# States kept as 64 by 48 blocks per head, with states and outputs computed in 64x64 array tiles

## The chip, the cores and the metric

The kernel runs on one core of a Trainium2 chip. The metric is the device time of one execution in microseconds (us). A run that is more than 1.5% above the fastest run of the same kernel is called slow here, the others fast, and ratios use fast runs alone.

Engine names in the profile lines: PE is the matrix engine (TensorE), PEld its weight loads, DVE is VectorE, ACT is ScalarE, POOL is GpSimd, SP is SyncE. A "q" behind the name means the sequencer of that engine, as when it issues a DMA. L929 is line 929 of the kernel that the profile belongs to.

## The reference

Two parts follow each other. Gated linear attention keeps a 48 by 48 state for each batch and head, and a dense block with a squared ReLU follows. All inputs and outputs are fp32. The sizes are B = 4 batches, H = 8 heads, S = 768 steps, D = 48.

```python
state = np.zeros((B, H, D, D))
for t in range(S):
    state = alpha[:, :, t, :, None] * state + einsum('bhd,bhe->bhde', k[:, :, t], v[:, :, t])
    y[:, :, t] = einsum('bhd,bhde->bhe', q[:, :, t], state)
x = y.transpose(0, 2, 1, 3).reshape(3072, 384)
h = np.maximum(x @ w_in, 0.0)          # w_in 384 x 2048
out = (h * h) @ w_out                  # w_out 2048 x 384
```

## The kernel before

The 3072 tokens are worked off in 12 units of 256 tokens: 3 stages in time, 4 batches in each. Within a unit, the recurrence is written as matrix products. For each unit TensorE computes, in this order: the decays (sums of log alpha), transposes of q and k, the scores, then one "output block", then the two large dense products of the MLP (L929 with `w_in`, L965 with `w_out`). A list scheduler in Python fixes the order of the instructions on each engine when the kernel is built. A list called `ORDER` tells it in which order the attention parts come, and it fits the dense work of earlier units in between.

The change and the argument are about the output block. It has up to three parts: "inter" (q times the state so far), "PM x V" (masked scores times v), and the state products k times v of the next unit. In the kernel before, two heads form a pair. Keys of a pair fill 128 rows of the array, so the product k times v of a pair is 128 by 96, of which only the two 48 by 48 blocks on the diagonal are wanted. A multiply with the mask `own` clears the rest. TensorE uses array tiles of 128x64 for inter and of 64x128 for the other two:

```python
def state_mm(g):                      # next states: 64x128 tiles, 96 columns
    ...
    for p in range(NPR):              # 4 pairs of heads
        for j in range(2):
            for c in range(1 if last else 2):
                h0 = 64 * c
                ins = pe.matmul(banks[c][:, p * 96:p * 96 + 96],
                                QKS[qs][h0:h0 + 64, 0, j, 2 * p:2 * p + 2, :].rearrange("p h d -> p (h d)"),
                                VBF[vb][h0:h0 + 64, 2 * p:2 * p + 2, j, :], ...)

def output_mm(g):
    ...
    for c in range(2):                # inter: 128x64 tiles, 96 columns
        state = SMD[x2] if c else SBD[sr]
        ...
        for p in range(NPR):
            for j in range(2):
                pe.matmul(psX[64 * j:64 * j + 64, c, p * 96:p * 96 + 96],
                          KQT[kt][:, 1, j, p, 64 * c:64 * c + 64], state[:, p * 96:p * 96 + 96], ...)
    for h in range(H):                # PM x V: 64x128 tiles, 48 columns
        for jk in range(2):
            for c in range(2):
                n, rr_ = h // 2, h % 2
                ins = pe.matmul(psX[:, c, h * D:(h + 1) * D],
                                PM[pm][64 * c:64 * c + 64, n // 2, rr_, n % 2, jk, :],
                                VBF[vb][64 * c:64 * c + 64, h, jk, :], ...)
...
# state update (DVE and POOL), 384 columns
add("dve", lambda e: e.tensor_tensor(TMP[0][:], ps0, SBD[sr][:], ALU.add), ...)
add("pool", lambda e: e.tensor_tensor(sm3, hd(TMP[0][:]), own, ALU.mult), ...)
...
ORDER = ["f0", "k0", "p0", "f1", "y0", "p1", "k1", "y1", "f2", "p2", "k2"]
for g in range(3, G):                 # f: front, p: scores, k: states, y: output,
    ORDER += [f"f{g}", f"w{g - 1}", f"p{g}"]     # w: output with the next unit's states
```

## Time and profile before

| | before |
|---|---|
| median of the timed runs | 179.53 us (179.25 to 180.75, 3 runs); 179.84 us with a fourth, run beside the changed kernel |
| span of the profiled execution | 179.8 us (its own time was 181.48 us, above all of the timed ones) |
| TensorE busy | 173.1 us, 96% |
| VectorE / ScalarE busy | 121.6 us / 118.8 us |
| matmuls, and as many weight loads | 2301 |
| first dense product | at 19.1 us |

These lines are from the page of before: busy time, share and number of instructions of each engine; the queue that fetches instructions, with packets, MB and share of the DMA engines' time; the chain of waits by engine; and two groups of instructions (line, engine, operation, tensors, shape, count, then busy us and mean ns of one, then the idle time before them).

```profile
PE 173.1 (96%) x2301; PEld 137.8 (77%) x2301; DVE 121.6 (68%) x192; ACT 118.8 (66%) x215; POOL 28.2 (16%) x36
...
q8 instruction: 18, 0.29, 0.7%
...
PE 85%; DMA 10%; SPq 2%; issue 1%; ACT 0%
...
L796 DVE TENSOR_TENSOR tmp<-psZ,sbd 128x384 f32<-128x384 f32 x8 | 4.4, 554 | 5.4 <-PE psZ L743 5.4
...
L770 PE MATMUL psX<-vbf,pm 64*128 64x48 bf16 x384 | 6.9, 180 | 0.0
```

TensorE is the bound: it is busy 96% of the time and has 85% of the chain. The state add on DVE takes 554 ns, but DVE is busy for only 68%. The line of q8 looks like a line to skip. It says that TensorE's instructions reached it in 18 packets of 16 KB (0.29 MB over 18). That q8 is TensorE's own queue is read from the counts: 4637 TensorE instructions in the trace go with 18 packets here, and 5265, 6033 and 6241 with 20, 23 and 24 in runs below, about one packet for every 256.

The next lines are the timeline of TensorE in before around one output block: start, length, engine, line, operation, tensors, array tile, shape, count.

```profile
93.01 0.60 PE L929 MATMUL psWH<-xt,win 128*128 128x256 bf16 x4
93.54 0.36 PE L763 MATMUL psX<-sbd,kqt 128*64 128x96 bf16 x8
93.74 0.34 PE L763 MATMUL psX<-smd,kqt 128*64 128x96 bf16 x8
94.01 0.58 PE L770 MATMUL psX<-vbf,pm 64*128 64x48 bf16 x32
94.42 0.50 PE L743 MATMUL psZ<-vbf,qks 64*128 64x96 bf16 x16
94.86 0.44 PE L929 MATMUL psWH<-xt,win 128*128 128x256 bf16 x2
```

Lengths overlap (one matmul of PM x V is recorded with some 180 ns, and the next pair starts 25 ns after it), so starts are what to compare. PM x V takes from 94.01 to 94.42, that is 32 matmuls in 0.41 us, 26 ns for each pair of tiles. The block has 64 matmuls. With the changes of array mode (by the starts, 94 ns at its head, 96 ns before PM x V and 93 ns at its end) it costs 1.47 us beyond the dense streams around it (in a dense stream a matmul of 256 columns follows every 109 ns in this trace, one of 384 columns every 162 ns).

The last lines are from the chain of waits of before, in order of time (start, length, what):

```profile
108.81 1.09 PE psWH L929 x11
109.91 3.92 DMA xt<-xbf
...
113.87 0.88 PE psWH L929 x6
```

In this execution the first dense product of unit 7 waits for a transpose made by DMA. TensorE stands still for 1.1 us at 112.6 us.

### The profile page before, as it was taken

To read this page: it belongs to the slowest core of one execution; us is meant where nothing else is said; L and a number is where in the kernel's file an instruction comes from. 1 tells how busy PE (TensorE), PEld (TensorE's weight loads), DVE (VectorE), ACT (ScalarE), POOL (GpSimd) and SP (SyncE) were. 2 spreads that over 40 slices of the span, in tenths; PEclk is the share of its full clock that TensorE was granted. 3 is DMA by queue.
4 is the path that set the end of the run, shared out by engine and by line. 5 is a ranking of instruction groups with operands and counts; after the bars stand their busy time and mean duration, and the time that the engine had idled before them with its cause. 6 is when DMAs were issued, how large, how long until landed. Compare 5 with 4: busy or idle time off the path is not lost.

```text
span 179.8 us, 5243 instructions
## 1 busy us (share of the span) xinstructions
PE 173.1 (96%) x2301; PEld 137.8 (77%) x2301; DVE 121.6 (68%) x192; ACT 118.8 (66%) x215; POOL 28.2 (16%) x36
## 2 busy tenths in 40 slices
PE   7989899999999999999999999799999999999994
PEld 5868698866787788878878788678878788788773
DVE  6569488698877997997998829773728745424130
ACT  4673399478767859949888639756549554656441
POOL 3250750022020021323405300500000000000000
PEclk9999999999999999999999999999999999999999
DMA  5999999999999999999999999756122941130112
GB/s 127 278 250 193 227 264 211 237 270 252 215 281 225 272 269 189 300 234 319 247 180 284 232 246 266 179 104 146 46 55 60 142 44 47 44 91 0 44 47 88
DMA packets 74871, 32.39 MB, mean 180 GB/s; under 512 B 70336, under 2 KB 73536, under 8 KB 74848
## 3 DMA queue, kind: packets, MB, share of 16 engines
q1 hardware_dynamic: 71344, 27.34, 67.3%
q0 software_dynamic: 3504, 4.72, 14.0%
q8 instruction: 18, 0.29, 0.7%
q14 instruction: 5, 0.04, 0.1%
HBM read 25.17 MB, written 4.72 MB: 166 GB/s over the span
## 4 chain that ended last, share of the span: by engine, by line
PE 85%; DMA 10%; SPq 2%; issue 1%; ACT 0%
PE psWH L929 36%; PE psO L965 33%; DMA win<-in_moe_w_in_dram 5%; PE psX L770 3%; DMA raw<-in_alpha_dram 3%; PE psX L763 3%; DMA xt<-xbf 2%; PE psZ L743 2%; PE psX L826 2%; SPq L511 2%; PE psX L899 1%; PE psZ L826 1%; PE psX L872 1%; PE psWH L630 1%; PE psO L1009 1%
## 5 line engine op out<-in xcount | busy, mean ns | idle before, releaser
L929 PE MATMUL psWH<-xt,win 128*128 128x256 bf16 x576 | 74.1, 275 | 1.8 <-DMA xt<-xbf 1.0
L929 PEld LDWEIGHTS psWH<-xt,win 128*128 128x128 bf16 x576 | 65.1, 145 | 7.0 <-DMA xt<-xbf 1.3
L965 PE MATMUL psO<-wout,gt 128*128 128x384 bf16 x368 | 68.9, 326 | 0.1
L937 ACT ACTIVATE rr<-psWH 128x512 bf16<-128x512 f32 x86 | 51.1, 596 | 24.9 <-PE psWH L929 23.1
L965 PEld LDWEIGHTS psO<-wout,gt 128*128 128x128 bf16 x368 | 34.8, 98 | 18.3 <-ACT osb L972 0.3
L947 DVE TENSOR_TENSOR gt<-rr 128x1024 bf16<-128x1024 bf16 (+1 forms) x44 | 27.3, 627 | 29.0 <-ACT rr L937 28.7
L972 ACT ACTIVATE osb<-psO 128x384 f32<-128x384 f32 x23 | 11.3, 493 | 14.4 <-PE psO L965 14.0
L839 DVE TENSOR_TENSOR pm<-psZ,caus 128x1024 bf16<-128x1024 f32 x12 | 14.6, 1217 | 2.6 <-PE psZ L826 2.6
L839 DVE TENSOR_TENSOR pm<-psX,caus 128x1024 bf16<-128x1024 f32 x12 | 14.6, 1218 | 1.7 <-PE psZ L826 1.5
L857 ACT ACTIVATE xbf<-psX 128x768 bf16<-128x768 f32 x11 | 8.9, 809 | 8.7 <-PE psZ L743 6.5
L951 ACT ACTIVATE gt<-rr 128x1024 bf16<-128x1024 bf16 (+1 forms) x16 | 13.9, 866 | 0.5 <-DVE rr L939 0.2
L623 POOL TENSOR_TENSOR prd<-raw 128x384 f32<-128x384 f32 x7 | 7.4, 1063 | 37.4 <-DMA raw<-in_alpha_dram 37.4
L1009 PE MATMUL psO<-zero 128*128 128x256 bf16 x74 | 11.7, 306 | 1.3 <-DVE zero L426 1.3
L693 DVE TENSOR_TENSOR qks<-raw,ek 128x768 bf16<-128x768 f32 x11 | 11.3, 1030 | 0.0
L693 DVE TENSOR_TENSOR qks<-raw,eq 128x768 bf16<-128x768 f32 x11 | 10.8, 985 | 0.0
L1009 PEld LDWEIGHTS psO<-zero 128*128 128x128 bf16 x74 | 7.6, 109 | 2.8 <-DVE zero L426 1.2
L689 POOL CAST vbf<-raw 128x768 bf16<-128x768 f32 x5 | 5.0, 995 | 20.2 <-DMA raw<-in_v_dram 20.2
L796 DVE TENSOR_TENSOR tmp<-psZ,sbd 128x384 f32<-128x384 f32 x8 | 4.4, 554 | 5.4 <-PE psZ L743 5.4
L939 DVE TENSOR_SCALAR rr<-psWH 128x512 bf16<-128x512 f32 x10 | 6.9, 689 | 1.3 <-PE psWH L929 0.9
L770 PE MATMUL psX<-vbf,pm 64*128 64x48 bf16 x384 | 6.9, 180 | 0.0
L770 PEld LDWEIGHTS psX<-vbf,pm 64*128 64x128 bf16 x384 | 5.6, 93 | 0.8
L642 ACT ACTIVATE ek<-psWH 128x384 f32<-128x384 f32 x10 | 4.9, 490 | 2.0 <-PE psWH L634 1.8
(118 smaller groups left out, 165.4 us busy)
## 6 DMA issues: line engine op xcount, KB each, us to landing
out_dram<-osb SPq DMA_DIRECT2D x23, 192.0 KB, 2.7
raw<-in_k_dram SPq DMA_DIRECT2D x11, 384.0 KB, 4.8
raw<-in_q_dram SPq DMA_DIRECT2D x11, 384.0 KB, 5.4
raw<-in_v_dram SPq DMA_DIRECT2D x10, 384.0 KB, 5.5
raw<-in_alpha_dram SPq DMA_DIRECT2D x10, 384.0 KB, 4.2
win<-in_moe_w_in_dram POOLq DMA_DIRECT2D x2, 768.0 KB, 9.7
wout<-in_moe_w_out_dram POOLq DMA_DIRECT2D x2, 768.0 KB, 9.2
raw<-in_alpha_dram SPq DMA_DIRECT2D x2, 192.0 KB, 3.2
```

The costliest lines, as they stand in the source:

```text
L623: alts={"pool": (lambda e: e.tensor_tensor(hd(PRD[la][:]), al(0), al(1), ALU.mult), pool_ns(HD))})
L693: add("dve", lambda e, a=a, E=E: e.tensor_tensor(QKS[qs][:, a, :, :, 0:D], RAW[r][:, 1 + a].rearrange("p h j d -> p j h d"), E[la][:].rear ...
L770: ins = pe.matmul(psX[:, c, h * D:(h + 1) * D], PM[pm][64 * c:64 * c + 64, n // 2, rr_, n % 2, jk, :], VBF[vb][64 * c:64 * c + 64, h, jk, ...
L839: add("dve", lambda e, hf=hf, psT=psT: e.tensor_tensor(PM[pm][:, hf].rearrange("p r n j t -> p (r n) (j t)"), psT[:, :, :].rearrange("p r ...
L857: add("act", lambda e: e.activation(XBF[x2][:], psX[:, :, 0:HD], AF.Copy), act_ns(2 * HD), p0 + 6100, reads=[("ps", "X", 0), ("ps", "X", 1 ...
L929: ins = pe.matmul(psH[hb][:, i * T:(i + 1) * T], WIN[:, kk, hidden(fj)], mov, start=(kk == 0), stop=(kk == KT - 1))
L937: add("act", lambda e, hb=hb, rr=rr: e.activation(rr, psH[hb], AF.Relu), act_ns(512), pu + 600, reads=[("ps", "H", hb)], writes=[("rr", rb ...
L947: add("dve", lambda e, dst=dst, sq=sq: e.tensor_tensor(dst, sq, sq, ALU.mult), 148 + k * 267, pu + 1200, reads=[("rr", rb, h) for h in ran ...
L951: "act": (lambda e, dst=dst, sq=sq: e.activation(dst, sq, AF.Square), act_ns(k * 512))})
L965: ins = pe.matmul(psS, GT[gt][:, fj, j, :], WOUT[:, fj, :], start=(fj == 0), stop=(fj == FT - 1))
L972: add("act", lambda e, ob=ob, psS=psS: e.activation(OSB[ob][:], psS, AF.Copy), act_ns(DM), ps_ + 700, reads=[keyS], writes=[("osb", ob)], ...
L1009: pr.fill(lambda pe: pe.matmul(psO[:, 0:256], ZERO[:, 0:128], ZERO[:, 0:256], skip_group_check=True), 109, min(o.start for o in pr.order[" ...
```

## The change

The intent is to spend no array time on the unwanted halves of the states. A state becomes a 64 by 48 block per head; the two heads of a pair stand above each other, so a state tile has 192 columns instead of 384, and the mask `own` is not needed. All three parts of the block run in 64x64 tiles, four at a time, which also saves the change of mode within the block (96 ns in the trace of before). The inter products are cut into two halves: in the second half each row tile uses the bank that the other one used in the first. A semaphore stands between the halves, and the next states are put in front of its wait, so that the wait costs little (in the four full blocks of after the next inter product starts 3 to 9 ns after the last state product).

In numbers, a full block goes from 64 matmuls to 128: inter 16 to 32, PM x V 32 to 64, states 16 to 32.

```diff
+    HS = HD // 2
-    PE_X = 7                                  # units from here on: x transposed by DMA
+    DMA_X = (8, 9, 10)
-    DENSE = {}
+    DENSE = {11: 11 * 13000 + 15500}
-    SBD = sb("sbd", [128, HD], BF16, 2 * B)
-    SMD = sb("smd", [128, HD], BF16, 2)
+    SBD = sb("sbd", [128, HS], BF16, 2 * B)
+    SMD = sb("smd", [128, HS], BF16, 2)
 ...                                           # selector matmul of the decays goes, v always cast on chip
 # states
-                    for c in range(1 if last else 2):
-                        ins = pe.matmul(banks[c][:, p * 96:p * 96 + 96], ...
+                    for c in range(halves):
+                        for x in range(2):
+                            ins = pe.matmul(banks[c][64 * x:64 * x + 64, p * D:p * D + D],
+                                            QKS[qs][h0:h0 + 64, 0, j, 2 * p + x, :],
+                                            VBF[vb][h0:h0 + 64, 2 * p + x, j, :], ...
 # outputs
+        def inter(pe, pairs):
+            for p in range(NPR):
+                for j in range(2):
+                    for x, c in pairs:
+                        ins = pe.matmul(psX[64 * j:64 * j + 64, c, h * D:h * D + D],
+                                        KQT[kt][64 * x:64 * x + 64, 1, j, p, 64 * c:64 * c + 64],
+                                        (SMD[x2] if c else SBD[sr])[64 * x:64 * x + 64, p * D:p * D + D], ...
+            return ins
         def run(pe):
+            inter(pe, ((1, 1),) if first else ((0, 0), (1, 1)))
             for h in range(H):
                 for jk in range(2):
-                    for c in range(2):
-                        ins = pe.matmul(psX[:, c, h * D:(h + 1) * D], PM[...jk, :], ...
+                    for j in range(2):
+                        for c in range(2):
+                            ins = pe.matmul(psX[64 * j:64 * j + 64, c, h * D:(h + 1) * D],
+                                            PM[...jk, 64 * j:64 * j + 64], ...
+            ins.then_inc(swap, 1)
+            swaps[0] += 1
+            if between:
+                between(pe)                    # next unit's states
+            pe.wait_ge(swap, swaps[0])
+            return inter(pe, ((0, 1),) if first else ((0, 1), (1, 0)))
 # state update: one DVE add of 192 columns, no mask
-            add("dve", ... e.tensor_tensor(TMP[0][:], ps0, SBD[sr][:], ALU.add) ...
-            add("pool", ... e.tensor_tensor(sm3, hd(TMP[0][:]), own, ALU.mult) ...
+            add("dve", ... e.tensor_tensor(SMD[x2][:], ps0, SBD[sr][:], ALU.add) ...
 ...
     ORDER = ["f0", "k0", "p0", "f1", "y0", "p1", "k1", "y1", "f2", "p2", "k2"]
-    for g in range(3, G):
+    ORDER += ["f3", "y2", "k3", "p3"]
+    for g in range(4, G):
```

`DMA_X`, `DENSE` and `ORDER` are changes of the order of work. They come with the change but could be made without it: units 7 and 11 are transposed on TensorE again, the dense work of unit 11 gets an earlier rank, and unit 3 gets its states in a block of its own.

## The prediction

> **What bounds the kernel now.** TensorE. The page gives PE 96% of the 179.8 us span at clock 0.9 to 1.0. In the chain of waits PE has 85%, the two dense products 69% (L929, L965); the rest is the start (first dense product at 19.1 us) and a DMA transpose of 3.9 us at 110 us. Start-to-start spacing of matmuls beyond columns/2.4 plus 2.5 ns sums to 16 us lost, 10 of them after 20 us: mostly array mode changes, and one stall of 1.1 us (112.6 us, L929 waits for the transpose of unit 7). DVE (68%) and ACT (66%) are off the chain after 20 us.
>
> **The block that changes**, by the timeline at 93.5 us (one output with the next states): dense stream ends 93.45, first state product 93.54 (94 ns drain, 22 ns uncovered weight load); 8 pairs of 128x64 tiles, 42 ns a pair; 96 and 14 ns of change to 64x128 tiles; 16 pairs of PM x V at 25 ns; 8 pairs of next states at 42 ns; 93 ns back to the full array, 58 ns of uncovered load. Sum 1.47 us, 0.38 of it changes. [...] 93 to 96 ns each.
>
> **The change.** All in 64x64 tiles, four at once. Scores run so already: sets of four every 56 ns, streaming 128 columns. With 48 columns a set is bound by the 25 ns floor seen in PM x V, or by the weight load, which I read as 24 to 27 ns (delay after the first set); I take 28 ns. [...] 24 ns for 64 columns against 13 for 128. New block: 117 + 4x28 + 16x28 + 8x28 (states) + about 50 waiting for the swap + 4x28 + 151 = 1.23 us: 0.24 saved where states lie between and a previous state exists (7 units): 1.7 us. Outputs without states between (0, 1, 2, 11) expose some 0.25 us of completion latency and lose up to 0.24 each, partly in idle time; the separate third state costs two more changes. The selector matmul goes: 0.2 us. Transposing units 7 and 11 on PE costs 2x0.33 us and removes the 1.1 us stall. Net 2.1 to 2.6 us on the critical path.
>
> Off it: state updates halve (DVE 554 to about 345 ns, by 1.11 ns a column between 384 and 768 columns), the multiply with "own" goes (557 ns DVE, 1041 POOL), V casts are added; DVE loses some 8 us of 121. That may shave the fills in the chain between 20 and 32 us (about 1 us).
>
> **Prediction: 176.9 us** (175.0 to 179.2). Faster by over 2%: 0.25; within 2%: 0.70; slower: 0.05.
>
> **What will show it.** State and PM matmuls in sets of four, 28 ns apart; one mode change in, one out; the output block 1.2 to 1.25 us; no wait of L929 on the transpose at 112 us; dense totals unchanged.
>
> **What would make it wrong.** Weight loads of four tiles not running together, or issue limiting at 8 instructions per 28 ns (highest rate seen: 4 per 25): sets at 50 ns would cost 0.7 us a unit, 7 in all. A swap wait far over 50 ns. The reordered start shifting dense work, or the transpose stall returning at unit 8.

The 1.23 us for the block (the terms as printed make 1.21) and the 176.9 us stand on readings of the trace of before, and on estimates for the 28 ns of a set (from the 24 to 27 ns that its author read there), the 50 ns at the swap and the 0.25 us where no states lie between, for which after showed 32 to 34 ns, 3 to 45 ns and 0.25 to 0.28 us. What it calls a drain is a gap in the trace: the first product of the block starts 203 ns after the last dense matmul, where dense ones follow every 109 ns, so 94 ns more; what the array does in that gap is not shown. "Columns/2.4 plus 2.5 ns" fits the spacing in the trace, 109 ns for 256 columns and 162 ns for 384. The 24 and 13 ns are of weight loads: at the heads of the two modes, at 93.54 and 94.00 us, the second pair of loads starts 25 ns after the first with 64 weight columns and 12 ns after it with 128.

## The result, and the profile after

Ratios here and below are the mean time of one kernel's fast runs over the mean time of the other's fast runs of the same rounds, so not quite the ratio of the medians quoted beside them.

| | before | after |
|---|---|---|
| median | 179.84 us (179.25 to 180.75, 4 runs) | 185.75 us (185.40 to 186.93, 4 runs) |
| ratio after/before | | 1.0336, 95% interval 1.027 to 1.0401 |
| span of the profiled execution | 179.8 us | 183.9 us |
| matmuls (and as many weight loads) | 2301 | 3004 |
| VectorE busy | 121.6 us | 115.5 us |

The change made the kernel 3.4% slower.

The same lines of the page, of after:

```profile
PE 174.0 (95%) x3004; PEld 138.9 (75%) x3004; DVE 115.5 (63%) x182; ACT 116.9 (64%) x207; POOL 25.1 (14%) x35
...
q8 instruction: 23, 0.38, 0.8%
...
PE 85%; DMA 7%; SPq 2%; ACT 2%; issue 2%
...
L766 PE MATMUL psX<-vbf,pm 64*64 64x48 bf16 x768 | 9.2, 187 | 0.1
...
L796 DVE TENSOR_TENSOR smd<-psZ,sbd 128x192 bf16<-128x192 f32 x8 | 2.8, 354 | 8.4 <-PE psX L753 8.4
```

The add of the states fell from 554 to 354 ns as predicted (345), and DVE is busy 6.1 us less. TensorE's busy time grew by only 0.9 us, so most of the lost time is time in which TensorE did nothing. "issue" in the chain grew from 1% to 2%. The fetch queue q8 now has 23 packets.

The timeline of TensorE in after around one output block:

```profile
95.58 0.88 PE L929 MATMUL psWH<-xt,win 128*128 128x256 bf16 x6
96.39 0.21 PE L753 MATMUL psX<-sbd,kqt 64*64 64x48 bf16 x1
...
96.53 0.68 PE L766 MATMUL psX<-vbf,pm 64*64 64x48 bf16 x64
97.04 0.44 PE L730 MATMUL psZ<-vbf,qks 64*64 64x48 bf16 x32
97.31 0.20 PE L753 MATMUL psX<-smd,kqt 64*64 64x48 bf16 x1
...
97.58 0.99 PE L929 MATMUL psWH<-xt,win 128*128 128x256 bf16 x7
```

The four tiles do run together: PM x V takes from 96.53 to 97.04, that is 16 sets of four in 0.51 us, 32 ns a set. The states take 34 ns a set, and the whole block costs 1.34 us beyond the dense streams instead of 1.47. So this block gained, but only half of what was predicted, and PM x V alone became longer (0.51 us instead of 0.41). Nothing here explains 5.9 us.

What explains most of it is seen elsewhere. These lines are four other stretches of TensorE's timeline in after; the bracket gives the idle time before the line and what the profile holds responsible.

```profile
27.83 0.24 PE L622 MATMUL psWH<-ones,lab 128*128 128x1 bf16 x4
29.07 0.52 PE L929 MATMUL psWH<-xt,win 128*128 128x256 bf16 x3 [1.00 <-ACT ek L630]
...
70.79 0.44 PE L872 MATMUL psX<-ident,xbf 128*128 128x128 bf16 x5
71.98 0.23 PE L872 MATMUL psX<-ident,xbf 128*128 128x128 bf16 x1 [0.75 <-issue]
...
84.90 0.83 PE L929 MATMUL psWH<-xt,win 128*128 128x256 bf16 x6
86.57 0.60 PE L929 MATMUL psWH<-xt,win 128*128 128x256 bf16 x4 [0.84 <-ACT rr L937]
...
99.93 0.83 PE L929 MATMUL psWH<-xt,win 128*128 128x256 bf16 x6
101.81 0.66 PE L929 MATMUL psWH<-xt,win 128*128 128x256 bf16 x4 [1.05 <-issue]
```

Look at the second pair. Six transposes of the same tile stand one after the other in the program. They read one buffer, five run, and the sixth comes almost a microsecond later. At 101.81 likewise the engine stands still for about a microsecond and the profile knows of nothing that it waited for. For two of the four the profile names a ScalarE instruction, but it infers that from the semaphore event that came last, and we shall see that the position of the pause doesn't depend on it.

The clue is a count. Take all of TensorE's instructions, weight loads too, in the order in which they start (6033 in after), and number them from 0. Each packet of q8 in the trace has 16384 bytes, and there are 23 of them for the 6033 instructions, again about one for every 256. The four pauses stand at numbers 961, 2497, 3009 and 3521, which lie 1536, 512 and 512 apart, all multiples of 256. So the instructions are taken to come in blocks of 256. In this table the instructions of after are cut into such blocks, at numbers that leave 193 when divided by 256. It is my reckoning from the records of the trace, with times in us.

| block of instructions | used from | to | in | q8 packet during it | next block starts | pause before it |
|---|---|---|---|---|---|---|
| 193 to 448 | 10.58 | 15.10 | 4.53 | 12.85 to 13.96 | 15.41 | 0.31 |
| 449 to 704 | 15.41 | 22.51 | 7.10 | 19.14 to 20.07 | 22.52 | none |
| 705 to 960 | 22.52 | 27.91 | 5.39 | 26.58 to 27.62 | 28.96 | 1.06 |
| 961 to 1216 | 28.96 | 39.52 | 10.55 | 32.70 to 33.67 | 39.52 | none |
| ... | | | | | | |
| 2241 to 2496 | 67.41 | 71.02 | 3.60 | 69.48 to 70.64 | 71.98 | 0.96 |
| 2497 to 2752 | 71.98 | 82.20 | 10.22 | 75.48 to 76.40 | 82.20 | none |
| 2753 to 3008 | 82.20 | 85.46 | 3.26 | 84.26 to 85.22 | 86.57 | 1.11 |
| 3009 to 3264 | 86.57 | 96.60 | 10.03 | 91.12 to 92.08 | 96.60 | none |
| 3265 to 3520 | 96.60 | 100.48 | 3.88 | 99.52 to 100.47 | 101.81 | 1.32 |

All four long pauses, and the short one at 15.1 us, fall exactly on the border of two blocks, and each ends 1.34 to 1.45 us after a packet of q8 has ended. After 19 us no pause of this size falls elsewhere. The reading is: TensorE used up a block before the next one was there. In before, any 256 instructions in a row after 19 us take at least 5.37 us from the first start to the last; in after they take as little as 1.07 us, because one full output block is itself 128 matmuls and 128 weight loads. The four long pauses add up to 4.45 us.

The page of the DMA engines of after in the window 99 to 102 us shows the packet, between others that fill the engines (packets, MB, share of 16 engines' time):

```profile
q1 hardware_dynamic: 2176, 0.82, 99.8%
q8 instruction: 1, 0.02, 2.0%
```

### The profile page after: what moved, and what is told of

It reads as the page before. It is cut to its first block, busy times and chain, and to the rows that moved or that the text cites. A ratio compares the mean times of both kernels' runs of the same rounds, so it can differ in the third digit from the quotient of the medians.

```text
span 183.9 us, 6620 instructions
## 1 busy us (share of the span) xinstructions
PE 174.0 (95%) x3004; PEld 138.9 (75%) x3004; DVE 115.5 (63%) x182; ACT 116.9 (64%) x207; POOL 25.1 (14%) x35
## 4 chain that ended last, share of the span: by engine, by line
PE 85%; DMA 7%; SPq 2%; ACT 2%; issue 2%
PE psWH L929 36%; PE psO L965 33%; DMA win<-in_moe_w_in_dram 5%; PE psX L766 4%; DMA raw<-in_alpha_dram 3%; PE psX L753 3%; PE psX L826 2%; SPq L503 2%; PE psZ L730 2%; PE psX L899 1%; PE psX L872 1%; PE psZ L826 1%; PE psWH L619 1%; ACT rr L937 1%; SPq L494 1%
## 5 line engine op out<-in xcount | busy, mean ns | idle before, releaser
L929 PE MATMUL psWH<-xt,win 128*128 128x256 bf16 x576 | 74.5, 275 | 3.8 <-issue 1.1
L965 PE MATMUL psO<-wout,gt 128*128 128x384 bf16 x368 | 68.2, 326 | 0.2 <-ACT osb L972 0.2
L937 ACT ACTIVATE rr<-psWH 128x512 bf16<-128x512 f32 x84 | 49.8, 596 | 21.7 <-PE psWH L929 20.0
L947 DVE TENSOR_TENSOR gt<-rr 128x1024 bf16<-128x1024 bf16 (+1 forms) x48 | 28.0, 588 | 30.0 <-ACT rr L937 29.6
L1010 PE MATMUL psO<-zero 128*128 128x256 bf16 x70 | 10.9, 304 | 1.3 <-DVE zero L423 1.3
L951 ACT ACTIVATE gt<-rr 128x1024 bf16<-128x1024 bf16 (+1 forms) x12 | 10.9, 913 | 1.8 <-DVE rr L939 1.7
L678 DVE TENSOR_TENSOR qks<-raw,eq 128x768 bf16<-128x768 f32 x11 | 11.2, 1016 | 0.7 <-ACT eq L654 0.7
L939 DVE TENSOR_SCALAR rr<-psWH 128x512 bf16<-128x512 f32 x12 | 8.2, 690 | 4.2 <-PE psWH L929 4.1
L766 PE MATMUL psX<-vbf,pm 64*64 64x48 bf16 x768 | 9.2, 187 | 0.1
L766 PEld LDWEIGHTS psX<-vbf,pm 64*64 64x64 bf16 x768 | 8.0, 107 | 0.3 <-issue 0.2
L796 DVE TENSOR_TENSOR smd<-psZ,sbd 128x192 bf16<-128x192 f32 x8 | 2.8, 354 | 8.4 <-PE psX L753 8.4
L753 PE MATMUL psX<-smd,kqt 64*64 64x48 bf16 x192 | 7.6, 191 | 0.3
```

The costliest lines, as they stand in the source:

```text
L678: add("dve", lambda e, a=a, E=E: e.tensor_tensor(QKS[qs][:, a, :, :, 0:D], RAW[r][:, 1 + a].rearrange("p h j d -> p j h d"), E.rearrange(" ...
L753: ins = pe.matmul(psX[64 * j:64 * j + 64, c, h * D:h * D + D], KQT[kt][64 * x:64 * x + 64, 1, j, p, 64 * c:64 * c + 64], (SMD[x2] if c els ...
L766: ins = pe.matmul(psX[64 * j:64 * j + 64, c, h * D:(h + 1) * D], PM[pm][64 * c:64 * c + 64, n // 2, x, n % 2, jk, 64 * j:64 * j + 64], VBF ...
L929: ins = pe.matmul(psH[hb][:, i * T:(i + 1) * T], WIN[:, kk, hidden(fj)], mov, start=(kk == 0), stop=(kk == KT - 1))
L937: add("act", lambda e, hb=hb, rr=rr: e.activation(rr, psH[hb], AF.Relu), act_ns(512), pu + 600, reads=[("ps", "H", hb)], writes=[("rr", rb ...
L947: add("dve", lambda e, dst=dst, sq=sq: e.tensor_tensor(dst, sq, sq, ALU.mult), 148 + k * 267, pu + 1200, reads=[("rr", rb, h) for h in ran ...
```

## The experiments

The theory, F (fetch): the block of 256 instructions that holds an output block is used up before the next block has been fetched. A first rival, O (order): the changed order of work (`ORDER`, `DMA_X`, `DENSE`) makes TensorE wait for data. A second, T (tiles): the 64x64 tiles themselves, or the swap, are slower than predicted in all blocks. Twelve kernels were run, in four batches; each batch has its own runs of before on the same chip.

### Shifting the blocks with empty instructions: shift208 and shift256

If the pauses come from the borders of blocks, instructions put in early should move the borders against the work. The edit adds 208 or 256 empty instructions to TensorE among the early fill matmuls (matmuls on zeros that keep the array busy before the first data is there):

```diff
                     last = o.fn(eng)
+                    if e == "pe" and o.name == "fill" and padded[0] < 208:
+                        k = min(4, 208 - padded[0])
+                        for _ in range(k):
+                            eng.nop(nofuse=True)
+                        padded[0] += k
```

> 208 empty instructions on TensorE among the idle fills before 19 us; all other work and its order as in the changed kernel. Fetch theory: TensorE's instructions arrive in blocks of 256 (16 KB), and the four pauses of about 1 us in the changed kernel (27.9, 71.0, 85.5, 100.5 us, at instructions 961, 2497, 3009, 3521, all of the same remainder modulo 256) are blocks that were used up faster (3.3 to 5.4 us) than the next one came. A small model of it puts the loss at 3 to 5.5 us unshifted and at 0.3 to 0.9 us with a shift of 208: about 4 us less than the changed kernel, 181 to 182.5 us. Rival theories (the new order and the extra PE transposes cost the time; the 64x64 sets and the swap waits cost it): no change, 185 to 187 us, and the pauses stay at the same instructions of the program.

> The control of the run before: 256 empty instructions, so that every instruction keeps its place within its block of 256. Fetch theory: the pauses come back at the same instructions of the program as in the changed kernel, and the time is that of the changed kernel (185 to 187 us) although this differs from the run before only by 48 more empty instructions in the idle start. If empty instructions as such help or hurt, this run and the one before agree.

Measured: shift208 185.81 us (184.29 to 187.35), ratio 1.0326 (1.0237 to 1.0415); shift256 186.48 us (184.78 to 187.11), ratio 1.0377 (1.03 to 1.0453); before 179.51 us in this batch.

This was a miss. The traces have 6033 TensorE instructions and 23 packets of q8, exactly as after has: the empty instructions didn't reach the chip. Both runs are therefore repeats of after. As repeats they have some use. The pauses stand at the same numbers in both, 2497, 3009 and 3521, and in the trace of shift256 at 961 too, with lengths between 0.5 and 1.9 us, so they are no accident of one execution. (The profiled run of shift208 was a slow one.)

### The order of work alone: sched_only

The kernel before gets only the changes of the order:

```diff
-    PE_X = 7
+    DMA_X = (8, 9, 10)
-    DENSE = {}
+    DENSE = {11: 11 * 13000 + 15500}
 ...
-    for g in range(3, G):
+    ORDER += ["f3", "y2", "k3", "p3"]
+    for g in range(4, G):
```

> The kernel before with the change's order of work alone (third state by itself ahead of its scores, transposes of units 7 and 11 on PE, the last dense block earlier); states and outputs as before. Theory that the order costs the time: at least 3 us slower than before. Fetch theory: within 1.5 us of before, no pause of 1 us after a fetch of instructions, because the output block keeps half the instructions; the stall on the transpose at 112 us gone, 0.7 us of PE transposes added.

Measured: 180.96 us (180.34 to 182.10), ratio 1.0098 (1.0022 to 1.0173). The trace has no pause at a block border, and 18 packets. The transposes of x on TensorE after 19 us went from 2.05 to 2.81 us, where the prediction had 0.66 us for two more units. So the order explains about 1% of the 3.4%, some 0.8 us of it by the transposes, and it doesn't make the pauses. Theory O has a part, but not the larger one.

### Shifting the blocks with real instructions: pad208 and pad256

The early fill matmuls of 256 columns are split in up to four of 64 columns until 208 or 256 instructions have been added. That adds next to no array work (the fills are busy for 10.9 us in after, 10.9 us in pad208 and 11.2 us in pad256), and it comes before the first dense product.

```diff
-    pr.fill(lambda pe: pe.matmul(psO[:, 0:256], ZERO[:, 0:128], ZERO[:, 0:256], skip_group_check=True), 109,
+    def filler(pe, n=1):
+        for m in range(n):
+            cut = slice(m * 256 // n, (m + 1) * 256 // n)
+            ins = pe.matmul(psO[:, cut], ZERO[:, 0:128], ZERO[:, cut], skip_group_check=True)
+        return ins
+    pr.fill(filler, 109,
 ...                      # when emitting: n up to 4 until PAD instructions have been added
+PAD = 208                # pad256: 256
```

> The shift again, with instructions that reach the chip (the empty ones of the two runs before did not: the trace counted as many TensorE instructions as in the changed kernel and 23 blocks): early fill matmuls of 256 columns split into four of 64, 208 instructions more before 19 us, nearly the same time in each fill. Fetch theory: pauses at the old four places (instructions 961, 2497, 3009, 3521 of the changed kernel) vanish or shrink below 0.4 us each, a pause elsewhere of up to 1 us is possible; time 2 to 4.5 us below the changed kernel (181.5 to 184). Rivals: the pauses stay and so does the time, 185 to 187 us.

> The control: 256 instructions more, split the same way, so that each later instruction keeps its place within its block. Fetch theory: pauses of 0.5 to 1.9 us come back at the same instructions (old number plus 256) each ending about 1.3 us after a block's packet; time as the changed kernel, 184.5 to 187 us, and 2 to 4 us slower than the run before. Rivals: the two padded runs agree within 0.7 us.

Measured: pad256 185.82 us (184.56 to 187.18), ratio 1.0324 (1.0269 to 1.038). The timeline of TensorE in pad256 (start, length, what, and idle time before it):

```profile
69.32 0.44 PE L881 MATMUL psX<-ident,xbf 128*128 128x128 bf16 x5
71.47 0.23 PE L881 MATMUL psX<-ident,xbf 128*128 128x128 bf16 x1 [1.71 <-issue]
...
86.05 0.49 PE L938 MATMUL psWH<-xt,win 128*128 128x256 bf16 x3 [0.83 <-ACT rr L946]
...
100.95 0.33 PE L938 MATMUL psWH<-xt,win 128*128 128x256 bf16 x1 [0.66 <-issue]
```

Shifted by a whole block, three of the four pauses are at the same work as in after (the same sixth transpose again), now at instruction numbers 2753, 3265 and 3777, that is 256 later. They last 1.93, 1.10 and 0.92 us. The fourth, at 961, is not there again.

pad208, shifted by 208, has none of these pauses. The timeline of TensorE in pad208 runs through where the pause at 85 us was:

```profile
83.39 1.49 PE L938 MATMUL psWH<-xt,win 128*128 128x256 bf16 x12
84.72 0.33 PE L628 MATMUL psWH<-lab,linc 128*128 128x384 bf16 x1
84.88 0.24 PE L631 MATMUL psWH<-ones,lab 128*128 128x1 bf16 x4
84.98 1.79 PE L974 MATMUL psO<-wout,gt 128*128 128x384 bf16 x10
```

This pair is the test between F and any cause tied to the work itself. Apart from how the early fills are cut up, the work, its order and its data are the same in after, pad256 and pad208. Only the place of the borders differs, and the pauses keep to the borders. F is shown for where the pauses come from. (Quick use alone doesn't make a pause: in pad208 a block is used up in 2.72 us from 56.71 us on and the next one is there, because its packet began at 56.68 us, as the block was entered.)

The time of pad208 is less clear. Its five runs took 184.94, 183.83, 186.36, 183.71 and 180.98 us (median 183.83; before 179.99 in this batch). Four of them are more than 1.5% above the fastest and therefore count as slow, so no ratio can be given. The profiled run, of 184.94 us, shows what took the place of the pauses (timeline of pad208, all engines):

```profile
101.55 0.52 ACT L659 ACTIVATE la<-raw 128x384 f32<-128x384 f32 x1 [2.21 <-DMA raw<-in_alpha_dram]
101.98 1.06 ACT L946 ACTIVATE rr<-psWH 128x512 bf16<-128x512 f32 x2
...
102.61 0.33 PE L938 MATMUL psWH<-xt,win 128*128 128x256 bf16 x1 [1.21 <-ACT rr L946]
```

The order of ScalarE's instructions is fixed when the kernel is built. A logarithm of alpha stands in it in front of two evictions of a dense product, alpha is not loaded yet, and TensorE waits for the evictions: 1.5 us here, and 1.0 and 0.7 us at 92 to 94 us, the first of them behind the logarithm of another unit. In this execution, part of what the fetch cost comes back as a wait for a load that was hidden in after. How often that happens over many runs, the single profile doesn't say.

### PM x V back in 64x128 tiles: pv128

Everything of the change stays, except that PM x V has 32 matmuls of 128 weight columns again. It moves behind both halves of inter, so that the swap is still covered by the next states. A full block then has 96 matmuls, 192 instructions.

```diff
-            (PM x V loop with j, 64x64 tiles)
-            ins.then_inc(swap, 1)
+            inter(pe, ((1, 1),) if first else ((0, 0), (1, 1))).then_inc(swap, 1)
             if between:
                 between(pe)
             pe.wait_ge(swap, swaps[0])
-            return inter(pe, ((0, 1),) if first else ((0, 1), (1, 0)))
+            inter(pe, ((0, 1),) if first else ((0, 1), (1, 0)))
+            for h in range(H):
+                for jk in range(2):
+                    for c in range(2):
+                        ins = pe.matmul(psX[:, c, h * D:(h + 1) * D],
+                                        PM[pm][64 * c:64 * c + 64, n // 2, x, n % 2, jk, :], ...)
+            return ins
```

> The changed kernel with PM x V back in 64x128 tiles (32 matmuls instead of 64), after both halves of the state products: the output block has 192 instructions instead of 256, one more mode change. Array time as in the changed kernel: 16 pairs at 25 ns and 110 ns of change against 16 sets at 32 ns. Fetch theory: no block of 256 is used up in under 4 us, pauses of over 0.5 us gone or one left, 181 to 183 us. Rivals: as the changed kernel or slower by the added mode changes, 185 to 188 us.

Measured: 182.17 us (180.60 to 182.36), ratio 1.0094 (1.0054 to 1.0134). There are 20 packets and no pause at a block border; any 256 instructions in a row now take at least 4.17 us. From 1.0336 to 1.0094, that is 2.4% of before's time or 4.3 us, goes with PM x V in 64x64 tiles (2.3% against pad256, measured beside it). That is about the sum of the four pauses, but in part by chance: pv128 also gained 0.9 us in the blocks, and lost 2.9 us in waits that after doesn't have (both below). The blocks after 19 us add up to 16.01 us, reckoned from the starts of the matmuls less the dense streams around them, against 16.95 us in after (a full block is 1.31 us instead of 1.34). So theory T has a part too, 0.9 us, and it is not the larger one.

The profile also shows the wait of pad208 again (timeline of pv128):

```profile
99.13 0.52 ACT L650 ACTIVATE la<-raw 128x384 f32<-128x384 f32 x1 [2.69 <-DMA raw<-in_alpha_dram]
99.56 1.06 ACT L936 ACTIVATE rr<-psWH 128x512 bf16<-128x512 f32 x2
...
100.19 0.44 PE L928 MATMUL psWH<-xt,win 128*128 128x256 bf16 x2 [1.69 <-ACT rr L936]
```

TensorE stands still for 2.0 us at 98.2 us, behind the same logarithm, and for 0.9 us at 31.4 us for a load of `w_out`. After has neither wait. This fits pauses that had been time in which a load could arrive, so that the gain of taking them away would be smaller than their sum; no run tests that alone.

### The remaining 1%: before2, oldsched, pv128_old, pv128_lm

The third batch asks what the remaining 0.9% of pv128 is, and how wide the noise is. before2 is the unchanged kernel. oldsched is after with the old order of work, pv128_old is pv128 with the old order of work, and pv128_lm is pv128 with the logarithm moved behind the next one in ScalarE's order, for every unit in which it stood ahead of it (five in the trace of pv128, not unit 10 alone as the expectation has it).

```diff
 # oldsched (on after) and pv128_old (on pv128)
-    DMA_X = (8, 9, 10)
+    DMA_X = (7, 8, 9, 10, 11)
-    DENSE = {11: 11 * 13000 + 15500}
+    DENSE = {}
-    ORDER += ["f3", "y2", "k3", "p3"]
-    for g in range(4, G):
+    for g in range(3, G):
 # pv128_lm (on pv128), after scheduling
+    act = pr.order["act"]
+    for o in [o for o in act if o.name.startswith("lm")]:
+        after = next(a for a in act if a.name == "ln" + o.name[2:])
+        if act.index(o) < act.index(after):
+            act.remove(o)
+            act.insert(act.index(after) + 1, o)
```

> The kernel before once more, unchanged, for a second profile. The prediction counted the removal of a stall of 1.1 us (a dense product waiting for the transpose of unit 7) that the first profile showed; that profiled run took 181.48 us, the timed ones 178.7 to 180.5 mostly. If the stall belongs to that run alone, this profile has none over 0.5 us between 50 and 160 us and a span near 178; if it belongs to the kernel, it is there again. No pause after a block of instructions in either case. Time within 0.5% of before.

> The changed kernel with the order of before (third state in the output block of unit 2, transposes on PE up to unit 6 only, last dense block at its old rank): 64x64 tiles, half states, swap wait and 256 instructions an output block stay. Theory that the order costs most: within 1% of before. Fetch theory: pauses of about 1 us remain, at other instructions, as the 256-instruction blocks lie elsewhere; 182.5 to 186 us.

> PM x V in 64x128 tiles (192 instructions an output block) and the order of before: 64x48 states and the swap wait are what is left of the change. Fetch theory with block times as read (full blocks 0.15 us shorter than before, outputs without states between 0.3 longer): no pause after a block of instructions, 178.5 to 181 us, within 0.7% of before. If the tiles or the swap themselves cost several us, 183 or more.

> The PM x V variant of the round before, with nothing changed but the place of one kind of instruction in ScalarE's order: the logarithm of unit 10's alpha now stands behind the logarithm that follows it, not ahead of two evictions of dense products. In the profile of the variant PE stood still for 2.0 us at 98 us, behind those evictions, which stood behind that logarithm, which waited for its load until 99.0. Theory: that stall shrinks to under 0.7 us, 1 to 2 us less than 182.2. If the stall is from something else it stays.

Measured (before 180.55 us, 178.90 to 181.93, in this batch):

| kernel | median (range), us | ratio (95%) | pauses at block borders in the trace |
|---|---|---|---|
| before2 | 180.30 (179.80 to 181.77) | 1.0013 (0.9957 to 1.007) | none |
| oldsched | 183.91 (182.96 to 185.79, one of five slow) | 1.0222 (1.0152 to 1.0292) | 0.53, 0.32, 0.57, 0.37, 0.69 us at 449, 705, 961, 2497, 3009 |
| pv128_old | 180.78 (180.44 to 181.01) | 1.0022 (0.9975 to 1.0068) | none |
| pv128_lm | 181.12 (179.38 to 183.65, two of five slow) | 0.9992 (0.9919 to 1.0065) | none |

First, before2 tells about the stall that the prediction wanted to remove. Its chain of waits at the place where the first profile had 3.92 us of DMA:

```profile
112.33 0.65 PE psO L965 x4
112.98 0.04 issue
113.03 0.88 PE psWH L929 x6
```

The stall of 1.1 us is not there; the matmuls of the two products are 0.2 us further apart than their streaming needs. The stall stands in one of two profiled executions, the slower one, and so is no fixed cost of the kernel.

Second, oldsched has other borders against the work, and the five pauses in the table stand again at numbers that leave 193 when divided by 256. The three after 22 us are shorter than in after, 1.6 us together. Three other waits, of 0.66, 0.49 and 0.82 us at 42, 116 and 174 us, stand elsewhere; pv128_old has the same three, so they are not the fetch. With the old order as with the new one, PM x V in 64x128 tiles takes the pauses away and gains 2.0% (1.0222 to 1.0022).

Third, going back to the old order of work gains 1.1% (after to oldsched) or 0.7% (pv128 to pv128_old), near to the 1.0% of sched_only. The first of these three figures also holds the change in the pauses, since they are shorter in oldsched.

Fourth, pv128_old differs from before by the small states, the 64x64 inter and state products and the swap, and by nothing in the order of work. Its ratio is 1.0022, with an interval that holds 1: this part of the change costs or gains nothing that can be measured here.

Fifth, moving the logarithm took the wait of 2.0 us away (0.48 us at 90.5 us remained) and brought pv128 from 1.0094 to 0.9992, in intervals that overlap. So part of what the new order costs in pv128 may be this wait. The span of the profiled run of pv128_lm is 177.6 us, but two of five runs were slow.

### Two combinations: best_a and best_b

best_a is pv128_old with the logarithm moved and the earlier rank of the dense work of unit 11 (`DENSE`). best_b is pv128_lm with all transposes of units 7 to 11 on DMA.

```diff
 # best_a (on pv128_old), with the reordering of pv128_lm as well
-    DENSE = {}
+    DENSE = {11: 11 * 13000 + 15500}
 # best_b (on pv128_lm)
-    DMA_X = (8, 9, 10)
+    DMA_X = (7, 8, 9, 10, 11)
```

> A version meant to beat both: 64x48 states, PM x V in 64x128 tiles, the order of before, with the earlier rank of the last dense block alone out of the change's order, and the logarithm's place mended. In the variant without these a wait of 0.8 us for a square stood at 172 us and one of 0.5 us at 114. If they go and nothing new comes: 0.8 to 1.3 us less than 180.8, 179.5 to 180, at best 0.5% under before. No pause after a block of instructions.

> The changed kernel with PM x V in 64x128 tiles, the logarithm's place mended, and units 7 and 11 transposed by DMA again; third state by itself and the last dense block's rank as in the change. Without the two PE transposes (about 0.35 us each) 0.7 us less than the 181.1 measured without this edit, 179.5 to 181; if the transposing DMAs, in a stretch where DMA is busy throughout, stall a dense product as the first profile of before showed (1.1 us), no gain.

Measured (before 180.46 us, 178.85 to 185.17, in this batch): best_a 180.66 us (179.22 to 182.61), ratio 0.9999 (0.9943 to 1.0055), two of its six runs slow; best_b 181.73 us (180.34 to 183.22), ratio 1.0073 (1.0018 to 1.0127), one of six slow. Neither beats before, and both medians lie above what was expected. In the trace of best_a (of a slow run) no pause stands at a block border; the wait at 172 us is gone and the one of 0.5 us is still there. Transposing on DMA didn't help best_b, so the transposes on TensorE are not all of the order's cost. The two kernels differ in `ORDER` alone, that is in the states of unit 3 by themselves, and the means of their fast runs are 180.25 and 181.57 us. So 1.3 us, 0.7%, goes with that line here (my 95% interval from these nine runs: 0.1 to 2.6 us); by what wait or work stays open.

## Why the prediction was wrong

The prediction was 176.9 us with a range of 175.0 to 179.2 us and a chance of 0.05 for slower. The measured median is 185.75 us.

**The step that failed.** The prediction named "issue limiting at 8 instructions per 28 ns" as a danger, and treated it as a rate: if the sets of four come every 28 ns, then instructions are no limit. The rate was nearly good. What failed was the unstated step that TensorE's instructions are always there. They come in blocks of 256, a full output block uses up 256 of them in little more than a microsecond (1.07 us from 96.39 us on in after, 4.2 ns for each), and the pauses then fall into the dense work behind it, where the prediction looked for no change at all. Four pauses made 4.45 us in the profiled run. Both counts needed for this were on the page of before and in the diff: 18 packets for 2301 matmuls and as many loads, and 64 more matmuls in each full block. What was not on the page is that a packet can come late, as four did in after: the trace of before shows no pause at a block border.

**Sizes in the block.** The block was predicted at 1.23 us and measured at 1.34 us (units 5 and 6), against 1.47 us before. The sets run every 32 to 34 ns instead of 28; over 32 sets that is 0.17 us. The wait at the swap was put at 50 ns and is small where states lie between: the next inter product starts 3 to 9 ns after the last state product in the four full blocks, and 34 to 45 ns after it where only half the states lie between. The exposed latency where no states lie between was put at 0.25 us and is 0.25 to 0.28 us; there the block grew, for example from 1.08 to 1.32 us in unit 11. The other blocks gained less or grew: of the four whose next unit needs only half the states, two are 0.08 and 0.10 us shorter than before and two 0.03 and 0.04 us longer. Over all blocks after 19 us, my sum from the starts of matmuls less the dense streams around them is 16.17 us before and 16.95 us after (this holds one block of 1.67 us that comes right behind the small products of the decays). The prediction had 1.7 us less for the blocks with a previous state and next states, and up to some 0.24 us more in each of four others. So the gain in the blocks was not there either: they cost 0.8 us more than before, 1.5 to 2.5 us more than the prediction had.

**The stall of 1.1 us.** The prediction counted its removal as gain. before2 doesn't have it. It should have been seen as doubtful, since the profiled run took 181.48 us and the timed ones 179.25 to 180.75 us.

**The order of work.** Two more transposes on TensorE were put at 0.66 us and measured at 0.76 us in sched_only. The order as a whole costs 0.7 to 1.1%, that is 1.3 to 2.0 us. Of the rest the prediction had only two more changes of mode for the separate third state; by best_a and best_b that separate state may be most of the rest, and its cause is not found.

**What was right.** The four tiles run together, with one change of mode at each end, of 93 to 96 ns as before. DVE's add fell to 354 ns (345 predicted), DVE lost 6.1 us (8 predicted), and the prediction was right that TensorE, not DVE, was the bound. The dense products' busy times are unchanged (74.1 and 68.9 us before, 74.5 and 68.2 us after). Dropping the selector matmul, put at 0.2 us, was not measured by itself.

The account of the 3.4%, by runs: 2.0 to 2.4% go with PM x V in 64x64 tiles (after to pv128, oldsched to pv128_old), 0.7 to 1.1% with the order of work, and 0.2% with an interval of -0.25 to 0.7% remain for the small states and the swap. By the trace of after, roughly: 4.45 us of pauses, 0.78 us of longer blocks (16.95 less 16.17) and 0.76 us of transposes make 6.0 us, where the medians differ by 5.9. The sum fits better than it should: the profiled executions of after and before2 differ by 5.0 us (183.9 and 178.9), so some 1 us of the parts is made up elsewhere.

What stays open: how many blocks TensorE holds ahead (no run measures it); why packets in the paused places began 2.1 to 4.1 us after their block's first instruction. Until 112 us the DMA engines of after are nearly full of loads (the times of their packets make 0.95 to 1.08 of the engines' time, stretch by stretch, against 0.65 from 112 to 130 us and 0.42 from 130 to 150 us), and later, for instance at 145.46 us, a packet began 2.19 us before the block was entered, and a block used up in 3.58 us made no pause. That fits a fetch delayed by other DMA traffic, but no run here changes the traffic alone, and the packet of pad208 that began without delay at 56.68 us did so while loads filled the DMA engines (1.11 from 40 to 60 us). Nor does the time in which a block is used up decide by itself: in after a block of 5.39 us has a pause behind it, and in pad208 one of 2.72 us has none.

## What to carry to other kernels

Instructions are to be counted as well as array time: a rewrite into more, smaller matmuls must be asked not only whether the engine can start them fast enough, but how quickly it uses up 256 of them, with weight loads counted (here the blocks in front of the four long pauses were used up in 3.3 to 5.4 us, though one of 2.72 us in pad208 had no pause behind it). A pause in mid-stream, for which the profile names "issue" or an engine that had long been done, is tested by putting a number of real instructions in front that is no multiple of 256 beside one that is: here three of the four pauses came back at the same work with 256 more in front (pad256) and none of them with 208 more (pad208), which is what pointed to the fetch. And a stall in one profile is not yet a stall of the kernel, so compare the profiled run's own time with the timed runs before counting on its removal.
